# One decode step on one core: V of both head groups in one matmul, row sums as a column of the outputs, output projections in two column tiles

## The chip, the cores and the metric

The kernel runs on one core of one Trainium2 chip. The metric is the device time of one execution in microseconds, the median of three runs. The profile is of one further execution, and carries that execution's own time.

## The reference, cut to what matters

One token for each of 8 batch entries passes through attention over a sliding window and through a gated feed-forward block; both read the same normalised input, and the result gates the one with the other.

```python
xn = layernorm(x)                                  # x: (8, 1, 512) bfloat16
q  = xn @ wq                                       # 32 heads of 128
k, v = the last 1024 positions of k_cache, v_cache # 8 KV heads, each shared by 4 query heads
p  = softmax(q @ k^T * 128**-0.5)
s  = (p @ v) @ wo                                  # 4096 -> 512
f  = (gelu(xn @ w_gate) * (xn @ w_up)) @ w_down    # 512 -> 1792 -> 512
y  = x + s * silu(f)
```

The caches give 8 batch entries x 8 heads x 1024 positions x 128 x 2 bytes, twice: 33.6 MB. wq and wo are 4.2 MB each, the three feed-forward weights 1.8 MB each. Everything has to come from HBM once.

## The kernel before, in words

**Loads.** All large loads are issued by SyncE, in program order, on one DMA queue: wo's first quarter (`wo_first`, line 106), all of wq (line 109), then K and V of one batch entry after the other in halves of 1 MB (`load_cache`, line 84), w_gate and w_up (line 438), w_down (line 441), and the last three quarters of wo (line 451), the last of them in three pieces of 5, 2 and 1 of its 8 slices `j`. K, V and the late weights share a ring of eight slots. x comes on ScalarE's queue in five pieces of 2, 2, 2, 1 and 1 rows (line 79).

**Head.** VectorE normalises x, TensorE transposes it (line 167) and spreads x itself, by a matmul with a 0/1 matrix (line 172), onto the partitions that the result will have; ScalarE keeps that as `x_res` (line 179). Then 32 matmuls make q (line 261), and q is rearranged into `qbd`, a block form of the queries (line 284).

**Loop over the batch.** For each batch entry, `turn_k` transposes K on VectorE (line 249), `scores` makes a 128 x 1024 score tile in PSUM (line 311), `softmax` takes the maximum, the exponential (line 333) and, with the same instruction, the row sums, into the column `sums[:, b]`. `turn_p` transposes the probabilities (line 344). `values` multiplies them with V (line 355): the 32 positions `c` are dealt onto four column tiles of the array, 32 columns each (`t = c % 4`), once for each of the two groups `g` of four KV heads, so 64 matmuls of 128 moving columns. `keep_o` copies the result to SBUF (line 368). `gather`, one entry later, adds the four tiles by matmuls with a selection matrix in float32: two for the outputs (line 376) and two of one column for the sums (line 380). After four entries `regroup` divides by the sums and lays the heads out for wo (lines 391 to 407). The schedule is the program's own order; each engine executes its instructions in that order:

```python
softmax(b); scores(b + 1, 0); gather(b - 1)
turn_k(b + 1, 1); scores(b + 1, 1)
turn_p(b); values(b); keep_o(b)
```

**Tail.** After `gather(7)` and `regroup(1)` come w_gate and w_up (line 465), the gelu (lines 475 to 488), and w_down: for each of 14 slices `j` of 128 rows four matmuls, one for each column tile, with 128 of the 512 output columns each (line 494). The gate `g_sb` follows (lines 502 to 506). Then wo in the same form, 32 slices of four matmuls (line 513), where the loop over the quarters `u` follows the order in which they arrive. At last `y` (line 521), `out_sb` (line 523), and one store of 32 runs of 256 bytes (line 525).

Of the kernel before, what the change touches and what calls it, by code (L numbers as in the profile page):

```python
# [7 lines left out]
ACT = mybir.ActivationFunctionType  # L8
ALU = mybir.AluOpType
AX = mybir.AxisListType  # L10
BF16 = mybir.dt.bfloat16
FP32 = mybir.dt.float32
# [4 lines left out]
RB = 4  # L17
# [4 lines left out]
def kernel(  # L22
# [13 lines left out]
    nc = tc.nc  # L36

    B, Sq, D = A_x.shape
    Hkv, Sk, Dh = A_k_cache.shape[1], A_k_cache.shape[2], A_k_cache.shape[3]
# [6 lines left out]
    P = nc.NUM_PARTITIONS  # L46
    NK = D // P
    HG = 4
    NG = Hkv // HG
    C = W * HG // P  # L50
    ROW = C * Dh
    FT = F // 4
    NJ = F // P
    DT = D // 4

    ctx.enter_context(tc.manual_schedule())
    consts = ctx.enter_context(tc.tile_pool(name="consts", bufs=1))
    keep = ctx.enter_context(tc.tile_pool(name="keep", bufs=1))
    two = ctx.enter_context(tc.tile_pool(name="two", bufs=2))
# [15 lines left out]


    x_sb = keep.tile([B, D], BF16, name="x_sb")
    for r, z in ((0, 2), (2, 4), (4, 6), (6, 7), (7, 8)):
        nc.scalar.dma_start(out=x_sb[r:z], in_=A_x.flatten_outer_dims()[r:z])  # L79

    def load_cache(cache, b, name):
# [10 lines left out]
    k_sb, v_sb = {}, {}  # L92
# [4 lines left out]
    def load_v(b):  # L97
# [21 lines left out]
        out=ident,  # L119
        in_=ident,  # L120
# [13 lines left out]
        out=xpad,  # L134
        in_=xpad,
# [8 lines left out]
    stats = keep.tile([B, nc.vector.BN_STATS_DIM], FP32, name="stats")  # L144
# [3 lines left out]
    rstd = keep.tile([B, 1], FP32, name="rstd")  # L148
# [4 lines left out]
        out=xhat,  # L153
# [3 lines left out]
        op0=ALU.subtract,  # L157
        op1=ALU.mult,
    )
    x_res = keep.tile([P, DT], FP32, name="x_res")  # L160
    warm = keep.tile([B, 1], FP32, name="warm")
    nc.scalar.activation(out=warm, in_=rstd, func=ACT.Exp)  # L162
    with tc.tile_pool(name="ps_x", bufs=1, space=PSUM) as ps_x:
        xnT_ps = ps_x.tile([P, NK, B], BF16, name="xnT_ps")
        xv = xhat.rearrange("b (p k) -> b k p", k=NK)
        for k in range(NK):
            nc.tensor.transpose(xnT_ps[:, k, :], xv[:, k, :], ident[0:B, 0:B])  # L167
        for j in range(4):
            nc.vector.tensor_copy(out=xnR[:, :, j, 0 : RB * B : RB], in_=xnT_ps)
        xr_ps = ps_x.tile([P, DT], FP32, name="xr_ps")  # L170
        for t in range(4):
            nc.tensor.matmul(
                xr_ps[32 * t : 32 * t + 32, :],
                xpad,
                x_sb[:, t * DT : (t + 1) * DT],
                start=True,
                stop=True,
            )
        nc.scalar.copy(out=x_res, in_=xr_ps)  # L179
# [10 lines left out]
        out=hv,  # L190
        in_=hv,
# [7 lines left out]
        out=neg_st,  # L199
        in_=neg_st,  # L200
# [8 lines left out]
        out=neg_mv,  # L209
        in_=neg_mv,  # L210
# [9 lines left out]
    sel = consts.tile([P, NG, Hq], FP32, name="sel")  # L220
    nc.vector.memset(sel, 0.0)
    for g in range(NG):
        nc.vector.tensor_reduce(
            out=sel[:, g, g * qd : (g + 1) * qd],
            in_=ident.rearrange("p (t g h) -> p g h t", t=4, g=NG)[:, g],
# [5 lines left out]
        out=own, in_=ident.rearrange("p (i e) -> p e i", e=8), axis=AX.X, op=ALU.add  # L231
    )
    pick = consts.tile([P, 4 * NU], BF16, name="pick")
    with nc.allow_low_precision(reason="sums of zeros and a single one"):
        nc.vector.tensor_reduce(
            out=pick, in_=ident.rearrange("p (a e) -> p a e", e=8), axis=AX.X, op=ALU.add
# [20 lines left out]
    with tc.tile_pool(name="ps_q", bufs=1, space=PSUM) as ps_q:  # L257
        q_ps = [ps_q.tile([P, 512], FP32, name=f"q_ps{i}") for i in range(8)]
        for k in range(NK):
            for i in range(8):  # L260
# [4 lines left out]
                    start=(k == 0),  # L265
                    stop=(k == NK - 1),
                )
        for half in range(2):
            for i in range(4 * half, 4 * half + 4):
                e = nc.vector.tensor_copy if i % 4 == 3 else nc.scalar.copy  # L270
# [7 lines left out]
    for j in range(4):  # L278
        sl = slice(32 * j, 32 * j + 32)
        for m in range(2):  # L280
            for g in range(NG):
                e = nc.scalar.copy if (4 * j + 2 * m + g) % 3 == 2 else nc.vector.tensor_copy
# [3 lines left out]


    pT, S, P_sb, O_ps = {}, {}, {}, {}
    sums = keep.tile([P, B], FP32, name="sums")

    actx = ExitStack()
    ps_s = actx.enter_context(tc.tile_pool(name="ps_s", bufs=2, space=PSUM))
# [26 lines left out]
    def softmax(b):  # L319
        mx = two.tile([P, 1], FP32, name="mx")  # L320
        nc.vector.tensor_reduce(  # L321
            out=mx, in_=S[b].rearrange("p a c -> p (a c)"), axis=AX.X, op=ALU.max
        )

        m2 = two.tile([64, 1], FP32, name="m2")
        nc.vector.tensor_tensor(out=m2, in0=mx[0:64, :], in1=mx[64:128, :], op=ALU.max)
        m1 = two.tile([32, 1], FP32, name="m1")
        nc.vector.tensor_tensor(out=m1, in0=m2[0:32, :], in1=m2[32:64, :], op=ALU.max)  # L328
        nb = two.tile([P, 1], FP32, name="nb")
        for j in range(4):  # L330
            nc.scalar.mul(nb[32 * j : 32 * j + 32, :], m1, -inv)  # L331
        P_sb[b] = two.tile([P, C // 2, 32, 2], BF16, name="P_sb")
        nc.scalar.activation(  # L333
            out=P_sb[b].rearrange("p c i w -> p c w i"),
            in_=S[b].rearrange("p a (c w i) -> p (a c) w i", w=2, i=32),
            func=ACT.Exp,
            bias=nb,
            scale=inv,
            accum_out=sums[:, b : b + 1],
        )  # L340

    def turn_p(b):
        pT[b] = two.tile([P, C // 2, Hq, 2], BF16, name="pT")
        nc.vector.transpose(  # L344
            out=pT[b].rearrange("p c h w -> p (c h w)").bitcast(I32),
            in_=P_sb[b].rearrange("p c i w -> p (c i w)").bitcast(I32),
        )

    def values(b):
        O_ps[b] = ps_o.tile([P, NG, Dh], FP32, name="O_ps")  # L350
        for g in range(NG):
            vv = v_sb[b][:, g].rearrange("p (c d) -> p c d", d=Dh)
            for c in range(C):
                t = c % 4
                nc.tensor.matmul(  # L355
                    O_ps[b][32 * t : 32 * t + 32, g, :],
                    pT[b][:, c // 2, :, c % 2],
                    vv[:, c, :],
                    start=(c < 4),
                    stop=(c >= C - 4),  # L360
                )

    o_ps = {}
    O_sb = {}

    def keep_o(b):
        O_sb[b] = two.tile([P, NG, Dh], FP32, name="O_sb")
        nc.scalar.copy(out=O_sb[b], in_=O_ps[b])  # L368

    def gather(b):  # L370
        q = b % 4
        if q == 0:
            o_ps[b // 4] = ps_g.tile([P, Dh + 1], FP32, name="o_ps")
        o = o_ps[b // 4][32 * q : 32 * q + 32, :]
        for g in range(NG):
            nc.tensor.matmul(  # L376
                o[:, 0:Dh], sel[:, g, :], O_sb[b][:, g, :], start=(g == 0), stop=(g == NG - 1)
            )
        for g in range(NG):
            nc.tensor.matmul(  # L380
                o[:, Dh : Dh + 1],
                sel[:, g, :],
                sums[:, b : b + 1],
                start=(g == 0),
                stop=(g == NG - 1),
            )

    def regroup(q):

# [53 lines left out]
    for u in range(1, NU):  # L443
        if u % 2 == 1:
            pair = slot("wo_sb").rearrange("p (v j d) -> p v j d", v=2, d=D)
        t = pair[:, (u - 1) % 2]
# [5 lines left out]
        wo.append(t)  # L452

    gather(B - 1)
    regroup(1)
    actx.close()

    ps_f = ctx.enter_context(tc.tile_pool(name="ps_f", bufs=1, space=PSUM))
    ffn = ctx.enter_context(tc.tile_pool(name="ffn", bufs=1))
    zu = []  # L460
    for n, ws in (("z_ps", wgu[0]), ("u_ps", wgu[1])):
        ps = ps_f.tile([P, FT], FP32, name=n)
        for k in range(NK):
            for t in range(4):
# [4 lines left out]
                    start=(k == 0),  # L469
                    stop=(k == NK - 1),  # L470
# [6 lines left out]
        out=z2, in0=z2, scalar1=0.044715, scalar2=1.0, op0=ALU.mult, op1=ALU.add  # L477
# [10 lines left out]
    nc.vector.transpose(  # L488
        out=hT.rearrange("p j b -> p (j b)"), in_=h_bf.rearrange("p (y j) -> p j y", j=NJ)
    )  # L490
    f_ps = ps_f.tile([P, DT], FP32, name="f_ps")
    for j in range(NJ):
        for t in range(4):
            nc.tensor.matmul(
                f_ps[32 * t : 32 * t + 32, :],
                hT[:, j, :],
                wd[:, j, t * DT : (t + 1) * DT],
                start=(j == 0),
                stop=(j == NJ - 1),
            )  # L500
    g_sb = ffn.tile([P, DT], FP32, name="g_sb")
    nc.scalar.activation(out=g_sb, in_=f_ps, func=ACT.Tanh, scale=0.5)
    nc.vector.tensor_scalar(
        out=g_sb, in0=g_sb, scalar1=0.5, scalar2=0.5, op0=ALU.mult, op1=ALU.add
# [1 line left out]
    nc.vector.tensor_tensor(out=g_sb, in0=g_sb, in1=f_ps, op=ALU.mult)  # L506


    s_ps = ps_f.tile([P, DT], FP32, name="s_ps")
    for u in range(NU):  # L510
        for j in range(8):
            for t in range(4):
                nc.tensor.matmul(  # L513
                    s_ps[32 * t : 32 * t + 32, :],
                    oT[:, j, u, :],
                    wo[u][:, j, t * DT : (t + 1) * DT],
                    start=(u == 0 and j == 0),
                    stop=(u == NU - 1 and j == 7),
                )
    y = ffn.tile([P, DT], FP32, name="y")  # L520
    nc.vector.tensor_tensor(out=y, in0=s_ps, in1=g_sb, op=ALU.mult)
    out_sb = ffn.tile([P, DT], BF16, name="out_sb")
    nc.vector.tensor_tensor(out=out_sb, in0=y, in1=x_res, op=ALU.add)
    out_f = out.flatten_outer_dims()
    nc.sync.dma_start(
        out=out_f.rearrange("b (t d) -> t b d", t=4), in_=out_sb[0 : P : RB, :]
    )


# [28 lines left out]
```

## Time and profile before

| | |
|---|---|
| median of 3 runs | 120.95 us (120.84 to 121.92) |
| the profiled execution's own time | 120.88 us |
| its span in the profile | 119.0 us |
| mean granted TensorE clock | 0.887 |
| HBM read | 47.46 MB |
| busy: TensorE, VectorE, ScalarE | 61%, 64%, 26% of the span |
| SyncE's DMA queue | 94.6% of 16 engines' span |
| instructions | 2306, 992 of them matmuls |

Times in the trace are microseconds from the start of the span. "Idle before, releaser" is the time for which an engine did nothing ahead of an instruction, and what ended it. PEclk is the granted TensorE clock as a share of full speed. The matmuls' ends are modelled, their starts are recorded.

### The profile page before, as it was taken

To read this page: it belongs to the slowest core of one execution; us is meant where nothing else is said; L and a number is where in the kernel's file an instruction comes from. 1 tells how busy PE (TensorE), PEld (TensorE's weight loads), DVE (VectorE), ACT (ScalarE), POOL (GpSimd) and SP (SyncE) were. 2 spreads that over 40 slices of the span, in tenths; PEclk is the share of its full clock that TensorE was granted. 3 is DMA by queue.
4 is the path that set the end of the run, shared out by engine and by line. 5 is a ranking of instruction groups with operands and counts; after the bars stand their busy time and mean duration, and the time that the engine had idled before them with its cause. 6 is when DMAs were issued, how large, how long until landed. Compare 5 with 4: busy or idle time off the path is not lost.

```text
span 119.0 us, 2306 instructions
## 1 busy us (share of the span) xinstructions
PE 72.0 (61%) x992; PEld 37.5 (32%) x992; DVE 75.8 (64%) x101; ACT 31.4 (26%) x75; POOL 3.2 (3%) x10
## 2 busy tenths in 40 slices
PE   0000079941599596979964875698399264844650
PEld 0000033410133253545532434244135253414530
DVE  1000487999999999999957995971994224165100
ACT  1300230096202417170531421151070800120000
POOL 2000052000000000000000000000000000000000
PEclk9999999999679999999999999689859955578595
DMA  2998999999999999999999999999999999999930
GB/s 72 458 507 375 391 421 424 435 427 427 427 430 419 424 435 419 427 430 416 432 424 424 421 430 427 419 435 421 427 424 427 440 434 430 419 431 416 415 138 3
DMA packets 6109, 47.60 MB, mean 400 GB/s; under 512 B 716, under 2 KB 852, under 8 KB 1108
## 3 DMA queue, kind: packets, MB, share of 16 engines
q1 hardware_dynamic: 6084, 47.46, 94.6%
q8 instruction: 7, 0.11, 0.3%
q14 instruction: 2, 0.02, 0.0%
q10 hardware_dynamic: 16, 0.01, 0.0%
HBM read 47.46 MB, written 0.01 MB: 399 GB/s over the span
## 4 chain that ended last, share of the span: by engine, by line
DMA 61%; DVE 15%; PE 15%; ACT 3%; issue 2%; ACTq 1%; DVEq 0%
DMA wo_sb<-in_A_wo_dram 19%; DMA k_sb<-in_A_k_cache_dram 17%; DMA v_sb<-in_A_v_cache_dram 17%; DMA x_sb<-in_A_x_dram 9%; PE q_ps L261 7%; PE S_ps L311 6%; DVE kT L249 6%; DVE qbd L284 2%; DVE mx L321 2%; DVE q_both L274 1%; ACT P_sb L333 1%; ACTq L79 1%; ACT L162 1%; DVE q_both L271 1%; PE O_ps L355 1%
## 5 line engine op out<-in xcount | busy, mean ns | idle before, releaser
L311 PE MATMUL S_ps<-kT,qbd 128*128 128x512 bf16 x128 | 34.8, 420 | 15.4 <-DVE kT L249 12.0
L249 DVE STREAM_TRANSPOSE kT<-k_sb 128x2048 int32<-128x2048 int32 x16 | 36.6, 2289 | 5.0 <-DMA k_sb<-in_A_k_cache_dram 4.9
L311 PEld LDWEIGHTS <-qbd 128*128 128x128 bf16 x128 | 13.0, 103 | 33.3 <-issue 18.0
L331 ACT ACTIVATE nb<-m 32x1 f32<-32x1 f32 x32 | 6.4, 201 | 22.9 <-DVE m L328 22.6
L333 ACT ACTIVATE P_sb<-S_ps,nb 128x1024 bf16<-128x1024 f32 x8 | 11.1, 1391 | 0.3
L355 PE MATMUL O_ps<-v_sb,pT 128*32 128x128 bf16 x512 | 9.5, 231 | 2.6 <-DVE pT L344 2.6
L321 DVE TENSOR_REDUCE mx<-S_ps 128x1 f32<-128x1024 f32 x8 | 9.6, 1195 | 1.7 <-PE S_ps L311 1.6
L355 PEld LDWEIGHTS <-pT 128*32 128x32 bf16 x512 | 8.0, 103 | 5.6 <-issue 3.0
L261 PE MATMUL q_ps<-wq_sb,xnR 128*128 128x512 bf16 x32 | 9.2, 460 | 0.5 <-ACT x_res L179 0.5
L167 PE MATMUL xnT_ps<-ident,xhat 8*128 8x8 bf16 x4 | 0.3, 174 | 15.0 <-DVE xhat L152 15.0
L368 ACT COPY O_sb<-O_ps 128x256 f32<-128x256 f32 x8 | 3.0, 372 | 23.7 <-PE O_ps L355 23.7
L145 DVE BATCH_NORM_STATS2 stats<-x_sb 8x6 f32<-8x512 bf16 x1 | 0.7, 683 | 11.8 <-DMA x_sb<-in_A_x_dram 11.8
L344 DVE STREAM_TRANSPOSE pT<-P_sb 128x512 int32<-128x512 int32 x8 | 5.7, 711 | 3.4 <-ACT P_sb L333 3.3
L376 PE MATMUL o_ps<-O_sb,sel 128*32 128x128 f32 x32 | 5.4, 296 | 1.0 <-ACT O_sb L368 1.0
L300 PE MATMUL S_ps<-neg_mv,neg_st 128*128 128x512 bf16 x16 | 4.8, 381 | 1.9 <-DVE q_both L271 1.9
L261 PEld LDWEIGHTS <-xnR 128*128 128x128 bf16 x32 | 3.6, 114 | 5.8 <-issue 3.0
L271 ACT CAST q_both<-q_ps 128x512 bf16<-128x512 f32 x6 | 3.0, 613 | 7.9 <-PE q_ps L261 7.9
L167 PEld LDWEIGHTS <-xhat 8*128 8x128 bf16 x4 | 0.2, 114 | 15.0 <-DVE xhat L152 15.0
L376 PEld LDWEIGHTS o_ps<-O_sb,sel 128*32 128x32 f32 x32 | 3.0, 115 | 4.7 <-issue 3.2
L513 PE MATMUL s_ps<-wo_sb,oT 128*32 128x128 bf16 x96 | 2.7, 252 | 2.2 <-DMA wo_sb<-in_A_wo_dram 2.2
L252 DVE MEMSET qbd<- 128x4096 uint32 x1 | 3.5, 3472 | 0.8 <-issue 0.8
L513 PEld LDWEIGHTS <-oT 128*32 128x32 bf16 x128 | 3.0, 123 | 2.8 <-issue 2.6
(65 smaller groups left out, 51.1 us busy)
## 6 DMA issues: line engine op xcount, KB each, us to landing
k_sb<-in_A_k_cache_dram SPq DMA_DIRECT2D x16, 1024.0 KB, 19.7
v_sb<-in_A_v_cache_dram SPq DMA_DIRECT2D x16, 1024.0 KB, 19.8
wq_sb<-in_A_wq_dram SPq DMA_DIRECT2D x1, 4096.0 KB, 14.2
wo_sb<-in_A_wo_dram SPq DMA_DIRECT2D x2, 1024.0 KB
wgu_sb<-in_B_w_gate_dram SPq DMA_DIRECT2D x1, 1792.0 KB
wgu_sb<-in_B_w_up_dram SPq DMA_DIRECT2D x1, 1792.0 KB
wd_sb<-in_B_w_down_dram SPq DMA_DIRECT2D x1, 1792.0 KB, 25.1
wo_first<-in_A_wo_dram SPq DMA_DIRECT2D x1, 1024.0 KB, 4.8
```

What stands on the lines that cost most here:

```text
L249: nc.vector.transpose(out=t.bitcast(I32), in_=k_sb[b][:, g].bitcast(I32))
L261: nc.tensor.matmul(q_ps[i], xnR[:, k, :, :].rearrange("p j b -> p (j b)"), wq_sb[k][:, i * 512 : (i + 1) * 512], start=(k == 0), stop=(k = ...
L271: e(out=q_bf[:, i * 512 : (i + 1) * 512], in_=q_ps[i])
L300: nc.tensor.matmul(S[b][:, half, :], neg_st.rearrange("p j h -> p (j h)"), neg_mv.rearrange("p a n -> p (a n)"), start=True, stop=False,)
L311: nc.tensor.matmul(S[b][:, half, :], qbd[:, m, b, w, g, :], kv[:, half * 16 : (half + 1) * 16, m, :, w], start=False, stop=(g == NG - 1 an ...
L321: nc.vector.tensor_reduce(out=mx, in_=S[b].rearrange("p a c -> p (a c)"), axis=AX.X, op=ALU.max)
L331: nc.scalar.mul(nb[32 * j : 32 * j + 32, :], m1, -inv)
L333: nc.scalar.activation(out=P_sb[b].rearrange("p c i w -> p c w i"), in_=S[b].rearrange("p a (c w i) -> p (a c) w i", w=2, i=32), func=ACT.Exp,
L344: nc.vector.transpose(out=pT[b].rearrange("p c h w -> p (c h w)").bitcast(I32), in_=P_sb[b].rearrange("p c i w -> p (c i w)").bitcast(I32),)
L355: nc.tensor.matmul(O_ps[b][32 * t : 32 * t + 32, g, :], pT[b][:, c // 2, :, c % 2], vv[:, c, :], start=(c < 4), stop=(c >= C - 4),)
L376: nc.tensor.matmul(o[:, 0:Dh], sel[:, g, :], O_sb[b][:, g, :], start=(g == 0), stop=(g == NG - 1))
L513: nc.tensor.matmul(s_ps[32 * t : 32 * t + 32, :], oT[:, j, u, :], wo[u][:, j, t * DT : (t + 1) * DT], start=(u == 0 and j == 0), stop=(u = ...
```

## The change

1. **x in four pieces** of two rows each instead of five.
2. **Values.** One matmul of 256 moving columns (both head groups side by side) replaces two of 128: 32 for each batch entry instead of 64. The four column tiles stay.
3. **Sums.** `O_sb` becomes 129 columns wide for each group. The exponential writes its row sums straight into the last column of group 0, a new ScalarE copy of 128 x 1 puts them in group 1, `keep_o` fills the other columns, and `gather` needs two matmuls of 129 columns instead of two of 128 and two of one. `O_sb` is therefore taken from its two buffers in `softmax(b)`, no longer in `keep_o(b)`.
4. **w_down, wo and the result in two column tiles.** `DT` is 256 instead of 128: `x_res`, `f_ps`, `g_sb`, `s_ps`, `y` and `out_sb` have 64 partitions of 256 columns, and each slice `j` takes two matmuls of 256 columns instead of four of 128.
5. **The store** is two plain ones of 8 runs of 512 bytes, one issued by SyncE, one by ScalarE.
6. The table load ahead of the first exponential is drawn by an activation that writes into `stats` instead of a tile of its own.

```diff
-    DT = D // 4
+    NT = 2
+    DT = D // NT
-    for r, z in ((0, 2), (2, 4), (4, 6), (6, 7), (7, 8)):
+    for r, z in ((0, 2), (2, 4), (4, 6), (6, 8)):
         nc.scalar.dma_start(out=x_sb[r:z], in_=A_x.flatten_outer_dims()[r:z])
...
-    nc.scalar.activation(out=warm, in_=rstd, func=ACT.Exp)
+    nc.scalar.activation(out=stats[:, 0:1], in_=rstd, func=ACT.Exp)
...
+        O_sb[b] = two.tile([P, NG, Dh + 1], FP32, name="O_sb")
         nc.scalar.activation(out=P_sb[b]..., func=ACT.Exp,
-            accum_out=sums[:, b : b + 1],
+            accum_out=O_sb[b][:, 0, Dh : Dh + 1],
         )
+        nc.scalar.copy(out=O_sb[b][:, 1, Dh : Dh + 1], in_=O_sb[b][:, 0, Dh : Dh + 1])
...
-        for g in range(NG):
-            vv = v_sb[b][:, g].rearrange("p (c d) -> p c d", d=Dh)
-            for c in range(C):
-                t = c % 4
-                nc.tensor.matmul(O_ps[b][32 * t : 32 * t + 32, g, :],
-                    pT[b][:, c // 2, :, c % 2], vv[:, c, :], ...)
+        vv = v_sb[b].rearrange("p g (c d) -> p c g d", d=Dh)
+        for c in range(C):
+            t = c % 4
+            nc.tensor.matmul(O_ps[b][32 * t : 32 * t + 32, :, :],
+                pT[b][:, c // 2, :, c % 2], vv[:, c, :, :], ...)
...
-        nc.scalar.copy(out=O_sb[b], in_=O_ps[b])
+        nc.scalar.copy(out=O_sb[b][:, :, 0:Dh], in_=O_ps[b])
...
-            nc.tensor.matmul(o[:, 0:Dh], sel[:, g, :], O_sb[b][:, g, :], ...)
-        for g in range(NG):
-            nc.tensor.matmul(o[:, Dh : Dh + 1], sel[:, g, :], sums[:, b : b + 1], ...)
+            nc.tensor.matmul(o, sel[:, g, :], O_sb[b][:, g, :], ...)
...
     for j in range(NJ):
-        for t in range(4):
+        for t in range(NT):
             nc.tensor.matmul(f_ps[32 * t : 32 * t + 32, :], hT[:, j, :], wd[:, j, t * DT : (t + 1) * DT], ...)
...
     for u in range(NU):
         for j in range(8):
-            for t in range(4):
+            for t in range(NT):
                 nc.tensor.matmul(s_ps[32 * t : 32 * t + 32, :], oT[:, j, u, :], wo[u][:, j, t * DT : (t + 1) * DT], ...)
...
-    nc.sync.dma_start(
-        out=out_f.rearrange("b (t d) -> t b d", t=4), in_=out_sb[0 : P : RB, :]
-    )
+    for t, e in ((0, nc.sync), (1, nc.scalar)):
+        e.dma_start(
+            out=out_f[:, t * DT : (t + 1) * DT], in_=out_sb[32 * t : 32 * t + 32 : RB, :]
+        )
```

More of the change, by code (lines that the diff above doesn't have):

```diff
@@ L159 @@
     )
-    x_res = keep.tile([P, DT], FP32, name="x_res")
-    warm = keep.tile([B, 1], FP32, name="warm")
-    nc.scalar.activation(out=warm, in_=rstd, func=ACT.Exp)
+    x_res = keep.tile([32 * NT, DT], FP32, name="x_res")
+    nc.scalar.activation(out=stats[:, 0:1], in_=rstd, func=ACT.Exp)
     with tc.tile_pool(name="ps_x", bufs=1, space=PSUM) as ps_x:
@@ L169 @@
             nc.vector.tensor_copy(out=xnR[:, :, j, 0 : RB * B : RB], in_=xnT_ps)
-        xr_ps = ps_x.tile([P, DT], FP32, name="xr_ps")
-        for t in range(4):
+        xr_ps = ps_x.tile([32 * NT, DT], FP32, name="xr_ps")
+        for t in range(NT):
             nc.tensor.matmul(
@@ L288 @@
     pT, S, P_sb, O_ps = {}, {}, {}, {}
-    sums = keep.tile([P, B], FP32, name="sums")
     actx = ExitStack()
@@ L350, in values @@
         O_ps[b] = ps_o.tile([P, NG, Dh], FP32, name="O_ps")
-        for g in range(NG):
-            vv = v_sb[b][:, g].rearrange("p (c d) -> p c d", d=Dh)
-            for c in range(C):
-                t = c % 4
[L355 to L360, printed above, removed]
-                )
+        vv = v_sb[b].rearrange("p g (c d) -> p c g d", d=Dh)
+        for c in range(C):
+            t = c % 4
+            nc.tensor.matmul(
+                O_ps[b][32 * t : 32 * t + 32, :, :],
+                pT[b][:, c // 2, :, c % 2],
+                vv[:, c, :, :],
+                start=(c < 4),
+                stop=(c >= C - 4),
+            )
     o_ps = {}
@@ L366, in keep_o @@
     def keep_o(b):
-        O_sb[b] = two.tile([P, NG, Dh], FP32, name="O_sb")
-        nc.scalar.copy(out=O_sb[b], in_=O_ps[b])
+        nc.scalar.copy(out=O_sb[b][:, :, 0:Dh], in_=O_ps[b])
     def gather(b):
@@ L375, in gather @@
         for g in range(NG):
-            nc.tensor.matmul(
-                o[:, 0:Dh], sel[:, g, :], O_sb[b][:, g, :], start=(g == 0), stop=(g == NG - 1)
-            )
-        for g in range(NG):
[L380 to L386, printed above, removed]
+            nc.tensor.matmul(o, sel[:, g, :], O_sb[b][:, g, :], start=(g == 0), stop=(g == NG - 1))
     def regroup(q):
@@ L490 @@
     )
-    f_ps = ps_f.tile([P, DT], FP32, name="f_ps")
+    f_ps = ps_f.tile([32 * NT, DT], FP32, name="f_ps")
     for j in range(NJ):
-        for t in range(4):
+        for t in range(NT):
             nc.tensor.matmul(
@@ L500 @@
             )
-    g_sb = ffn.tile([P, DT], FP32, name="g_sb")
+    g_sb = ffn.tile([32 * NT, DT], FP32, name="g_sb")
     nc.scalar.activation(out=g_sb, in_=f_ps, func=ACT.Tanh, scale=0.5)
@@ L506 @@
     nc.vector.tensor_tensor(out=g_sb, in0=g_sb, in1=f_ps, op=ALU.mult)
-    s_ps = ps_f.tile([P, DT], FP32, name="s_ps")
+    s_ps = ps_f.tile([32 * NT, DT], FP32, name="s_ps")
     for u in range(NU):
         for j in range(8):
-            for t in range(4):
+            for t in range(NT):
                 nc.tensor.matmul(
@@ L519 @@
                 )
-    y = ffn.tile([P, DT], FP32, name="y")
+    y = ffn.tile([32 * NT, DT], FP32, name="y")
     nc.vector.tensor_tensor(out=y, in0=s_ps, in1=g_sb, op=ALU.mult)
-    out_sb = ffn.tile([P, DT], BF16, name="out_sb")
+    out_sb = ffn.tile([32 * NT, DT], BF16, name="out_sb")
     nc.vector.tensor_tensor(out=out_sb, in0=y, in1=x_res, op=ALU.add)
     out_f = out.flatten_outer_dims()
-    nc.sync.dma_start(
-        out=out_f.rearrange("b (t d) -> t b d", t=4), in_=out_sb[0 : P : RB, :]
-    )
+    for t, e in ((0, nc.sync), (1, nc.scalar)):
+        e.dma_start(
+            out=out_f[:, t * DT : (t + 1) * DT], in_=out_sb[32 * t : 32 * t + 32 : RB, :]
+        )
 _INS = ['A_x', 'A_k_cache', 'A_v_cache', 'A_wq', 'A_wo', 'B_x', 'B_w_gate', 'B_w_up', 'B_w_down']
```

## The prediction

> **What bounds the kernel.** I read the page's slices first, then the queues, then the timeline of the tail.
>
> ```profile
> DVE  1000487999999999999957995971994224165100
> DMA  2998999999999999999999999999999999999930
> GB/s 72 458 507 375 391 421 424 435 427 427 427 430 419 424 435 419 427 430 416 432 424 424 421 430 427 419 435 421 427 424 427 440 434 430 419 431 416 415 138 3
> q1 hardware_dynamic: 6084, 47.46, 94.6%
> q8 instruction: 7, 0.11, 0.3%
> DMA 61%; DVE 15%; PE 15%; ACT 3%; issue 2%; ACTq 1%; DVEq 0%
> ```
>
> From the second to the last slice but two, the DMA engines are full; 94.6% of 119.0 us is 112.6 us of packets on SyncE's queue, between the first near 2 us and the last at 115.06 us. No compute engine is full. The chain of waits runs through x, q and K, but it only follows who released whom: a 1 MB half of K or V takes 19.7 us from issue to landing while the queue moves 1 MB in 2.45 us, so about seven more loads are queued ahead of it. An issue could come some 17 us later before an engine ran dry. So nothing inside the loop sets the end; the stream of 47.46 MB does, and what follows its last byte:
>
> ```profile
> 108.80 1.35 PE L494 MATMUL f_ps<-wd_sb,hT 128*32 128x128 bf16 x56 [3.33 <-DVE hT L488]
> 109.92 1.08 PE L513 MATMUL s_ps<-wo_first,oT 128*32 128x128 bf16 x32
> 110.78 1.08 PE L513 MATMUL s_ps<-wo_sb,oT 128*32 128x128 bf16 x32
> 112.92 0.63 PE L513 MATMUL s_ps<-wo_sb,oT 128*32 128x128 bf16 x32 [1.06 <-DMA wo_sb<-in_A_wo_dram]
> 114.47 0.46 PE L513 MATMUL s_ps<-wo_sb,oT 128*32 128x128 bf16 x20 [0.92 <-DMA wo_sb<-in_A_wo_dram]
> 115.11 0.57 PE L513 MATMUL s_ps<-wo_sb,oT 128*32 128x128 bf16 x12 [0.18 <-DMA wo_sb<-in_A_wo_dram]
> 115.73 0.29 DVE L521 TENSOR_TENSOR y<-s_ps,g_sb 128x128 f32<-128x128 f32 x1 [4.61 <-PE s_ps L513]
> 116.06 0.29 DVE L523 TENSOR_TENSOR out_sb<-y,x_res 128x128 bf16<-128x128 f32 x1
> 116.38 0.70 SPq L525 DMA_DIRECT2D out_dram<-out_sb  x1
> ```
>
> TensorE is ahead of the stream: it waits for each of the last wo pieces. The last wait ends at 115.44 us (the recorded start of the last four matmuls). From there: 0.24 matmuls, 0.29, 0.29, 0.70 issue, 0.6 to the first store packet (117.68), 0.17 of packets, 0.35 until SyncE sees it (118.21), and the program's closing.
>
> **Part by part, against the profiled 120.88 us** (0.07 under the median).
>
> *x in four pieces.* A two-row piece puts one row on each of two engines (packets at 6.479 and 6.482 us), a one-row piece goes to one (8.95, then 11.41; its completion write at 12.66). Each packet waits some 1.2 us behind a 32 KB packet of wq. With four pieces the last completion is that of today's fourth, 10.20 us, so x lands 2.46 us earlier. q gains only up to wq's landing at 15.09 us plus about 0.4 until an engine sees it, against a q start of 16.03: 0.5 us. It frees slots earlier, which a full queue can't use: 0.
>
> *V in 256 columns.* At full clock 64 matmuls of 128 columns on four tiles take 1.08 us: 16 rounds x 53 ns and 0.22 for the last to drain. New: 8 rounds x 107 ns and some 0.27. The columns stay the same: +0.05 us for an entry, inside the loop, 0 for the end. The first matmul now needs both halves of V. The last half of entry 7 is complete at 94.83 us and `values(7)` starts at 96.05; slack about 0.8 even with the time to see it.
>
> *Sums.* Gone are 32 one-column matmuls with their loads. In entry 7 the next scores start at 89.37 us, held by them for 0.2 us; after `gather(7)` they keep `rc` from 99.48 until 99.69. Both are on the chain from the last K to f_ps: that chain gains 0.37 and loses 0.05 to V, so f_ps starts at 108.48 instead of 108.80 (w_down is there at 107.62 + 0.4). The new 128x1 copy, about 0.2 us by the nb row (201 ns), follows the exponential on ScalarE; next there is keep_o, which waits for V 2.75 us in entry 7. Uncovered it would cost 0.2 of these 0.32. The new wait of the exponential for `gather(b-2)` is met before the scores it needs.
>
> *Two column tiles.* Here work is added. A round of four 128-column matmuls starts every 55 ns at full clock (112.972, 113.027, 113.082) and every 107 ns at half (32 matmuls, 109.92 to 110.78). Two tiles of 256 columns need two such rounds for each slice: 109 and 213 ns. 46 slices (14 of w_down, 32 of wo) go from 2.5 to 5.0 us at full clock, from 4.9 to 9.8 at half. The clock in the tail:
>
> ```profile
> 106.00:107.00 1.00, 0.00 (x0) 0.00 (x0) 0.97 (x2) 0.00 (x0) 0.00 (x0) 1.00 0.97 414
> 109.60:110.00 0.40, 0.40 (x27) 0.40 (x20) 0.00 (x0) 0.00 (x0) 0.00 (x0) 0.50 1.12 471
> 111.50:112.00 0.50, 0.36 (x16) 0.18 (x5) 0.00 (x0) 0.00 (x0) 0.00 (x0) 0.50 0.90 379
> 113.00:114.00 1.00, 0.55 (x32) 0.40 (x32) 0.00 (x0) 0.00 (x0) 0.00 (x0) 1.00 0.73 279
> ```
>
> The seventh column is the clock: full until 109.20, half until 112.62, full after. New, with the same changes: 0.72 us at full are 6.7 slices; f_ps done at 110.75; wo's first quarter at 112.46; the second, mostly at full, at 113.39; the third (there at 112.92) at 114.24; the piece of five waits for 114.47 as today. **TensorE just catches up, with 0.2 us to spare**, and only the last pair costs: 256 columns instead of 128, +0.05.
>
> The clock's steps, twelve in the trace, all lie whole multiples of 3.413 us after the first at 20.457 us. The Trainium skill (TensorE: Matmul & The Clock Gate, "What's actually happening") says that this window runs free and doesn't start with the kernel. By that rule the step at 112.62 can lie elsewhere in another execution, and the backlog show in the time; no trace here shows a second phase.
>
> *y and out_sb* have 256 elements for each partition. 128 take 292 ns, 448 take 621 (lines 479 to 485): 1.03 ns each, so 0.42 each, +0.26 us in all. Nothing hides it.
>
> *Stores.* The 32 runs cost 0.70 us of issue. The x loads of one or two rows cost 0.24 to 0.27, ScalarE's first 0.54, loads of 128 runs 0.33 to 0.5. For 8 runs the bounds are 0.24 and, with a cold ScalarE queue as dear as today's store, 0.70 and 0.24 more. I take 0.54, nearest being ScalarE's own first: -0.16. Old packets lie on four engines, eight of 15 to 18 ns on each: 0.17; one 512-byte packet lies between that and 46 ns (1024 bytes): -0.12. One more event that SyncE waits for at the end: +0.06.
>
> The Trainium skill (DMA: Bandwidth & Descriptors, "Specifications") puts the smallest transfer at full rate at 512 bytes, with a read-modify-write below; by it the change would win at the store. The trace differs: a 256-byte write took 15 to 18 ns against 46 for a 1024-byte read, so it has at most the 0.12 to give.
>
> *Instructions.* TensorE loses 382 matmuls and as many weight loads (256 V, 32 sums, 28 w_down, 64 wo, 2 x_res), of 992 pairs. Its code comes in the seven 16 KB packets of the instruction queue, each on another DMA engine. In the completion writes each throws its engine back by 1.41 us: the 16 writes of one load spread over 0.56 us at 29 us, and over 1.81 at 105. The last engine sets the end of the stream. About four packets remain; by the engines of the first four, whose writes went to 1.66, 1.57, 1.66 and 1.70, the last landing is 0.1 earlier. Bounds: -1.2 (no late engine), +0.2 (the last of the unhit ones is hit, 0.56 + 1.41).
>
> **Sum:** -0.10 stream, +0.05 last matmuls, +0.26 VectorE, -0.16 and -0.12 store, +0.06 event = -0.01. **120.9 us, no change**; its own range by the bounds of stream and store 120.4 to 121.4.
>
> **Rivals.**
>
> *TensorE becomes the last (slower).* It decides where the 43 slices due by 115.11 us don't fit into the 6.6 us after 108.48, that is, where over 4.1 us of these are at half clock; today's steps give 3.4. With other positions of the steps and a window counted as busy from about 75% on (2.66 of 3.41 us were followed by full clock, 2.44 by half), I get up to +0.75: 121.1 to 121.7. If the clock stayed at half throughout, 46 x 0.213 = 9.8 us end at 118.3 plus draining, 2.7 later: 123.6. Against it: the window ahead of 112.62 is filled better than before. For it: only 0.2 us to spare.
>
> *The stream ends earlier (faster).* If no packet of code hits an engine that is late already, up to 1.2 us: 119.7. Against: seven out of seven left their mark.
>
> *The loop was the bound after all,* as the chain has it: q's 0.5 us would reach the end, 120.4. Against: the full DMA row.
>
> *The change saves nothing on TensorE*, since 256 columns stream as long as two times 128. I hold that to be so; a gain from fewer instructions in the loop would need an idle DMA.
>
> **Chances.** Forecast 0.63; TensorE last for part of a window 0.15 (121.1 to 121.7); at half clock throughout 0.10 (123.6); stream earlier 0.07 (119.7); loop 0.03; a dearer second store 0.02 (122.2). A measurement of this kernel tells about 1% (1.2 us) from no change. Faster 0.07; slower 0.10 + 0.02 and 0.01 from the phases = 0.13; same 0.80. Range 120.2 to 121.9: it leaves out the stream's case, the half clock throughout and the store.
>
> **What would show it.** V 32 matmuls in some 1.1 us; q start near 15.5; f_ps starting near 108.5 and taking 2.3 to 2.6 us; wait for wo_sb ahead of the last pieces kept but shorter than 0.9; y and out_sb 0.42; issue under 0.55. Wrong, if the last matmuls wait for no DMA, or the last completion write moves by over 0.3 us.

## The result and the profile after

The changed kernel takes **121.43 us** (median of 22 runs, 121.20 to 121.85), the kernel before 120.94 us (median of 22). The ratio is 1.0033, with a 95% interval of 1.0019 to 1.0046: slower by 0.4 us in the ratio, 0.49 in the medians, where I had forecast no change.

From the page of the changed kernel, slices and queues as before:

```profile
DMA  2998999999999999999999999999999999999920
GB/s 69 459 506 374 393 420 426 437 423 426 426 431 417 423 434 428 423 420 437 428 417 423 434 420 428 426 437 423 417 431 431 436 442 419 428 420 423 403 83 3
q1 hardware_dynamic: 6064, 47.45, 94.4%
q8 instruction: 5, 0.08, 0.2%
DMA 60%; PE 23%; DVE 9%; ACT 3%; issue 1%; SPq 0%; DVEq 0%
```

The DMA engines are as full as before in every slice up to the last but two. The instruction packets (q8) went from seven to five. The chain of waits now has PE 23% where it had 15%: it no longer reaches the end through the last wo load, but through w_down's and wo's matmuls. The timeline of the tail says the same (start, duration, engine and line; in brackets idle time before and what ended it):

```profile
108.23 3.17 PE L483 MATMUL f_ps<-wd_sb,hT 128*32 128x256 bf16 x28 [2.82 <-DVE hT L477]
111.19 1.53 PE L502 MATMUL s_ps<-wo_first,oT 128*32 128x256 bf16 x16
112.56 3.02 PE L502 MATMUL s_ps<-wo_sb,oT 128*32 128x256 bf16 x48
115.62 0.42 DVE L510 TENSOR_TENSOR y<-s_ps,g_sb 64x256 f32<-64x256 f32 x1 [2.96 <-PE s_ps L502]
116.07 0.42 DVE L512 TENSOR_TENSOR out_sb<-y,x_res 64x256 bf16<-64x256 f32 x1
116.51 0.80 SPq L515 DMA_DIRECT2D out_dram<-out_sb  x1
116.52 0.75 ACTq L515 DMA_DIRECT2D out_dram<-out_sb  x1
```

Against the rows of before: wo's matmuls stand in one block without a marked wait for a load; `y` and `out_sb` take 0.42 us each instead of 0.29; the issue of a store takes 0.80 and 0.75 us, not the 0.54 of my estimate, and not even less than the 0.70 of before. f_ps's row takes 3.17 us, where I had said 2.3 to 2.6, since the clock in this execution was half until 112.20 us. The last byte of wo is complete at 114.95 us (115.06 before), the last two matmuls start at 115.29 (115.44), out_sb ends at 116.49 (116.35), and the span ends at 119.34 (119.02). So the changed kernel is 0.15 us ahead when TensorE sees the last load, 0.14 behind at the end of out_sb, and 0.32 behind at the end: **all of the loss lies behind the last load**, some 0.3 us in front of the store and some 0.2 in it. The store's part, from the end of out_sb on, is made up as follows: SyncE's issue 0.10 longer, its first packet 0.78 us after the issue's end instead of 0.61, its packets 0.09 shorter, and the rest, from its last completion write to the end of the span, as before. This profiled execution took 121.20 us and is one of the two fastest of the 22; why most take 0.2 us more is a question for the runs below.

### The profile page after: what moved, and what is told of

Read it like the earlier page. It is cut to its first block, busy times and chain, and to the rows that moved or that the text cites. A ratio compares the mean times of both kernels' runs of the same rounds, so it can differ in the third digit from the quotient of the medians.

```text
span 119.3 us, 1553 instructions
## 1 busy us (share of the span) xinstructions
PE 73.7 (62%) x610; PEld 35.1 (29%) x610; DVE 76.3 (64%) x101; ACT 33.1 (28%) x83; POOL 3.2 (3%) x10
## 4 chain that ended last, share of the span: by engine, by line
DMA 60%; PE 23%; DVE 9%; ACT 3%; issue 1%; SPq 0%; DVEq 0%
DMA k_sb<-in_A_k_cache_dram 48%; DMA wq_sb<-in_A_wq_dram 12%; PE q_ps L261 8%; PE S_ps L310 4%; PE s_ps L502 4%; PE f_ps L483 3%; DVE kT L249 2%; PE O_ps L355 2%; PE z_ps L454 1%; PE o_ps L375 1%; ACT P_sb L333 1%; DVE o_x L382 1%; DVE mx L320 1%; DVE hT L477 1%; ACT nb L330 1%
## 5 line engine op out<-in xcount | busy, mean ns | idle before, releaser
L355 PE MATMUL O_ps<-v_sb,pT 128*32 128x256 bf16 x256 | 9.3, 292 | 2.7 <-DVE pT L345 2.7
L355 PEld LDWEIGHTS <-pT 128*32 128x32 bf16 x256 | 6.5, 102 | 6.3 <-issue 3.0
L375 PE MATMUL o_ps<-O_sb,sel 128*32 128x129 f32 x32 | 5.5, 297 | 1.0 <-ACT O_sb L367 1.0
L483 PE MATMUL f_ps<-wd_sb,hT 128*32 128x256 bf16 x28 | 3.2, 419 | 2.8 <-DVE hT L477 2.8
L502 PEld LDWEIGHTS <-oT 128*32 128x32 bf16 x64 | 3.6, 107 | 0.9
```

Source lines behind the costliest of these rows:

```text
L355: nc.tensor.matmul(O_ps[b][32 * t : 32 * t + 32, :, :], pT[b][:, c // 2, :, c % 2], vv[:, c, :, :], start=(c < 4), stop=(c >= C - 4),)
L375: nc.tensor.matmul(o, sel[:, g, :], O_sb[b][:, g, :], start=(g == 0), stop=(g == NG - 1))
L483: nc.tensor.matmul(f_ps[32 * t : 32 * t + 32, :], hT[:, j, :], wd[:, j, t * DT : (t + 1) * DT], start=(j == 0), stop=(j == NJ - 1),)
L502: nc.tensor.matmul(s_ps[32 * t : 32 * t + 32, :], oT[:, j, u, :], wo[u][:, j, t * DT : (t + 1) * DT], start=(u == 0 and j == 0), stop=(u = ...
```

## The experiments

Two theories were to be told apart. S: the constant parts behind the last load, the wider `y` and `out_sb` and the two stores, make the loss. T: TensorE, with half of its column tiles, is late in part of the executions.

**One store instead of two** (changed kernel, SyncE alone).

```diff
-    for t, e in ((0, nc.sync), (1, nc.scalar)):
-        e.dma_start(out=out_f[:, t * DT : (t + 1) * DT], in_=out_sb[32 * t : 32 * t + 32 : RB, :])
+    nc.sync.dma_start(
+        out=out_f.rearrange("b (t d) -> t b d", t=NT), in_=out_sb[0 : 32 * NT : RB, :])
```

> The changed kernel with one store again, issued by SyncE: 16 runs of 512 bytes, both column tiles. Theory S (the stores): in the two profiles the stretch from the end of out_sb to the end of the span went from 2.67 to 2.85 us, where I had forecast 0.22 less. If the second store and its queue cost that, this run is 0.15 to 0.25 us under the changed kernel (121.43), near 121.2, and the stretch is 2.7 us or less. Theory T (TensorE late in part of the executions, by the position of the clock's steps): no change, 121.4, and executions spread as widely (0.4 us between most). If the issue costs 0.8 us whatever the store looks like, 121.4 too, but then the profile shows one issue of 0.8 us.

Measured: 121.22 us (11 runs), 1.0025 of before (1.0016 to 1.0034). 0.2 us under the changed kernel: S.

```profile
116.68 0.69 SPq L514 DMA_DIRECT2D out_dram<-out_sb  x1
```

The issue took 0.69 us with the same number of 512-byte runs, and from out_sb's end to the span's end it is 2.74 us (changed kernel: 2.86; before: 2.67). Of the 0.24 us left over before, 0.07 lie behind out_sb, most of it one more semaphore that SyncE looks at after the store's; the rest is not the store's.

**Two stores in the kernel before.**

```diff
-    nc.sync.dma_start(out=out_f.rearrange("b (t d) -> t b d", t=4), in_=out_sb[0 : P : RB, :])
+    for h, e in ((0, nc.sync), (1, nc.scalar)):
+        e.dma_start(
+            out=out_f[:, 2 * h * DT : 2 * (h + 1) * DT].rearrange("b (t d) -> t b d", t=2),
+            in_=out_sb[64 * h : 64 * h + 64 : RB, :])
```

> The kernel before with its store cut in two, one half issued by SyncE, one by ScalarE (16 runs of 256 bytes each), and nothing else. Theory S: 0.15 to 0.25 us above the kernel before, 121.1 to 121.2, with a first store packet later by 0.2 to 0.4 us. Theory T: no change, 120.95, since TensorE is ahead of the stream with four column tiles.

Measured: 121.28 us (12 runs), 1.0031 (1.0017 to 1.0046): +0.3, S again, and more than expected. Its tail, from the timeline:

```profile
115.84 0.29 DVE L521 TENSOR_TENSOR y<-s_ps,g_sb 128x128 f32<-128x128 f32 x1 [4.12 <-PE s_ps L513]
116.16 0.29 DVE L523 TENSOR_TENSOR out_sb<-y,x_res 128x128 bf16<-128x128 f32 x1
116.48 0.68 SPq L526 DMA_DIRECT2D out_dram<-out_sb  x1
116.48 0.64 ACTq L526 DMA_DIRECT2D out_dram<-out_sb  x1
```

Counted from out_sb's end, issues and packets are no later than with one store: the first store packets at 117.77 and 117.81 us, the last completion write at 118.00, 1.55 us after out_sb's end against 1.50 before. My expectation of a first packet later by 0.2 to 0.4 us was wrong. The time goes after that: SyncE sees the completion 0.50 us after the write (before: 0.36), and then has three more events to go through, 0.06 us each, since it waits for its semaphores in a fixed order and the store's was the last one in the kernel before. These three come to 0.16 us, about half of what this run lost; in the changed kernel the later store's semaphore is the last again, so that part says nothing about its loss.

**Everything but the two column tiles and the two stores.**

```diff
-    NT = 2
+    NT = 4
...
-    for t, e in ((0, nc.sync), (1, nc.scalar)):
-        e.dma_start(out=out_f[:, t * DT : (t + 1) * DT], in_=out_sb[32 * t : 32 * t + 32 : RB, :])
+    nc.sync.dma_start(
+        out=out_f.rearrange("b (t d) -> t b d", t=NT), in_=out_sb[0 : 32 * NT : RB, :])
```

> The changed kernel with four column tiles of 128 for w_down, wo, x_res and the result, and the one store of before; x in four pieces, V in 256 columns and the sums column stay. Both theories: the loss is gone. By the steps: the last byte lands 0.1 us earlier, nothing is added, 120.8 (120.6 to 121.0). If V, the sums or the new wait cost something in the loop after all, it stays above 121.1.

Measured: 121.00 us (11 runs), 1.0001 (0.9992 to 1.0009). The loss is gone, as both theories say; the 0.1 to 0.2 us of gain that I expected isn't there. Its timeline shows why four tiles don't care:

```profile
108.07 1.69 PE L483 MATMUL f_ps<-wd_sb,hT 128*32 128x128 bf16 x56 [2.57 <-DMA wd_sb<-in_B_w_down_dram]
109.52 1.09 PE L502 MATMUL s_ps<-wo_first,oT 128*32 128x128 bf16 x32
110.50 0.69 PE L502 MATMUL s_ps<-wo_sb,oT 128*32 128x128 bf16 x32
112.94 0.63 PE L502 MATMUL s_ps<-wo_sb,oT 128*32 128x128 bf16 x32 [1.75 <-DMA wo_sb<-in_A_wo_dram]
114.46 1.24 PE L502 MATMUL s_ps<-wo_sb,oT 128*32 128x128 bf16 x32 [0.89 <-DMA wo_sb<-in_A_wo_dram]
```

f_ps starts 0.7 us earlier than in the kernel before, now held by w_down's load, and TensorE waits 1.75 us for wo's third quarter instead of 1.06. The clock was full in the last scores of this profile and half in those of before, so not all of the 0.7 us need be the change's. V in 256 columns, the sums column and the earlier x buy idle time, nothing else. The last load is complete at 115.03 us, against 115.06.

**TensorE with room** (the changed kernel without wo's first quarter).

```diff
-    for u in range(NU):
+    for u in range(1, NU):
...
-                    start=(u == 0 and j == 0),
+                    start=(u == 1 and j == 0),
```

> The changed kernel without the 16 matmuls of wo's first quarter (that part of the projection is left out, its load stays): TensorE gets 0.9 to 1.7 us of room ahead of the last wo pieces, and nothing else changes. Theory T: the executions in which TensorE was late lose 0.1 to 0.5 us; median near 121.2, the value of the best executions of the changed kernel, and a spread as narrow as before's (0.2 us). Theory S: no change, 121.4.

Measured: 121.42 us (5 runs, 121.37 to 121.50), 1.0041 (1.0029 to 1.0053). No change of the median: **T falls as the cause of the median's loss.** TensorE now waits for each piece again:

```profile
113.01 1.05 PE L502 MATMUL s_ps<-wo_sb,oT 128*32 128x256 bf16 x16 [0.60 <-DMA wo_sb<-in_A_wo_dram]
114.52 1.22 PE L502 MATMUL s_ps<-wo_sb,oT 128*32 128x256 bf16 x16 [0.46 <-DMA wo_sb<-in_A_wo_dram]
```

The five runs spread over 0.13 us, the 22 of the changed kernel over 0.65, so the slowest executions may still be T's. The profiled execution of this run took 121.37 us: the last load is complete at 115.12 us, the last matmuls start at 115.45, out_sb ends at 116.64, and from there it takes 2.87 us. The changed kernel's profiled execution, 0.17 us faster, differs from it mainly in the last load (114.95), which is probably what made it one of the fastest.

**TensorE without room** (w_down's matmuls twice).

```diff
+    for again in range(2):
         for j in range(NJ):
             for t in range(NT):
                 nc.tensor.matmul(f_ps[32 * t : 32 * t + 32, :], ...)
```

> The changed kernel with w_down's 28 matmuls run twice into the same sums (the second pass starts over, so the result is the same): TensorE gets 14 more slices ahead of wo, 1.5 us at full clock, 3.0 at half. In the profile of the changed kernel TensorE reached the piece of five at 114.36 us with under 0.1 us of waiting. If TensorE stands at the edge there, nearly all of it appears in the time: 122.8 to 124.4, and no matmul waits for a wo load any more. If there was hidden room, less than 0.8 us appears.

Measured: 123.16 us (4 runs, 121.79 to 123.31), 1.0143 (1.0095 to 1.0191). Of some 2.2 us of additional matmuls (the row of w_down takes 5.34 us instead of 3.17), 1.7 reach the median; in one run of the four, 121.79 us, only 0.4 did. From its timeline:

```profile
108.53 5.34 PE L484 MATMUL f_ps<-wd_sb,hT 128*32 128x256 bf16 x56 [3.07 <-DVE hT L477]
113.70 1.04 PE L503 MATMUL s_ps<-wo_first,oT 128*32 128x256 bf16 x16
114.57 2.79 PE L503 MATMUL s_ps<-wo_sb,oT 128*32 128x256 bf16 x48
117.40 0.42 DVE L511 TENSOR_TENSOR y<-s_ps,g_sb 64x256 f32<-64x256 f32 x1 [2.28 <-PE s_ps L503]
```

No wo matmul waits for a load, and the last start at 117.08 us, while the last load is complete at 115.09. So T's mechanism is real, and in most executions its price begins right behind where the changed kernel stands. The run at 121.79 us hid over 1 us of the added work; there is no profile of it, but its mean granted clock, 0.900, was the highest of the four.

**A warm queue** (kernel before, with a small copy on SyncE's queue ahead of the store).

```diff
+    wk = ffn.tile([1, 64], FP32, name="wk")
+    nc.sync.dma_start(out=wk, in_=g_sb[0:1, 0:64])
     y = ffn.tile([P, DT], FP32, name="y")
```

> The kernel before, with one more issue on SyncE's queue some 4 us ahead of the store: 256 bytes of g_sb copied into a tile that nobody reads. Theory C (cold queue): the store's issue costs 0.70 us, where loads of x cost 0.24, because SyncE has issued nothing for 20 us; then it falls to 0.3 to 0.5 us and the time by 0.2 to 0.4, 120.6 to 120.8. Theory F (an issue of a store costs this much, whatever came before): still 0.70 us, 120.95, or a little more for one more completion to wait for.

Measured: 121.28 us (12 runs), 1.0019 (1.0007 to 1.0032). The small copy was issued at 111.48 us, 0.62 us long, and the store's issue is as it was:

```profile
111.48 0.62 SPq L521 DMA_DIRECT2D wk<-g_sb  x1
112.95 0.63 PE L513 MATMUL s_ps<-wo_sb,oT 128*32 128x128 bf16 x32 [0.77 <-DMA wo_sb<-in_A_wo_dram]
...
116.37 0.72 SPq L527 DMA_DIRECT2D out_dram<-out_sb  x1
```

A queue idle for 20 us is not the reason; theory C falls. The added 0.3 us is not the copy itself, long done: in the profile the stretch behind out_sb is 2.85 us instead of 2.67, as the store's semaphore again isn't the last in SyncE's order; the rest of the added time lies outside the span and stays unexplained. Three of the twelve runs, with the same span, took 120.92 to 120.95 us.

**The first store alone** (changed kernel, right half not written).

```diff
-    for t, e in ((0, nc.sync), (1, nc.scalar)):
+    for t, e in ((0, nc.sync),):
```

> The changed kernel with SyncE's store alone: the right half of the result is not written. If the second store costs by its own completion and by standing beside the first, the issue falls from 0.80 to 0.70 us or less, the stretch from the end of out_sb to the end of the span from 2.86 to 2.65, and the time to 121.2. If a store of 8 runs on eight engines is dear by itself, the issue stays at 0.8 us, and only the second completion (0.06 to 0.2 us) goes: 121.25 to 121.4.

Measured: 121.23 us (12 runs), 1.0021 (1.0010 to 1.0033). Mixed, as neither sentence foresaw:

```profile
116.78 0.80 SPq L515 DMA_DIRECT2D out_dram<-out_sb  x1
```

The issue stays at 0.80 us with nobody beside it, but the first packet comes 0.61 us after it again, the stretch falls to 2.74 us and the time by 0.2 us, the same as with one store of both halves. So the second store costs about 0.2 us, and the dear issue of the eight-engine store is paid back by its packets (first to last start in 0.06 us instead of 0.16).

This run's profile also holds a case of theory T (the columns of the stretches: their length, then busy time and instructions of PE, PEld, DVE, ACT and POOL, granted clock, DMA share, GB/s):

```profile
112.00:113.00 1.00, 1.00 (x14) 0.69 (x11) 0.41 (x1) 0.00 (x0) 0.00 (x0) 0.50 0.97 395
113.00:114.00 1.00, 1.00 (x18) 0.84 (x16) 0.00 (x0) 0.00 (x0) 0.00 (x0) 0.79 0.73 277
115.00:115.60 0.60, 0.60 (x16) 0.53 (x12) 0.00 (x0) 0.00 (x0) 0.00 (x0) 1.00 0.01 2
```

The full clock comes at 113.42 us, 1.2 us later than in the changed kernel's profile (112.20). TensorE is busy without a gap, the last matmuls start one pair after the other, 109 ns apart, until 115.57, although the last load was complete at 115.05 and would have let them start at 115.4. So this execution lost 0.1 to 0.2 us to TensorE: 121.35 us against a median of 121.23.

**The store on ScalarE's queue** (as the four-tile kernel above).

```diff
-    nc.sync.dma_start(
+    nc.scalar.dma_start(
         out=out_f.rearrange("b (t d) -> t b d", t=NT), in_=out_sb[0 : 32 * NT : RB, :])
```

> The changed kernel with four column tiles and one store, this store issued by ScalarE instead of SyncE. In the runs with two stores ScalarE's issue took 0.05 us less than SyncE's (0.64 against 0.68, 0.75 against 0.80). If that is all that differs, 0.05 us under the same kernel with SyncE's store (121.0), about 120.95, which a measurement can't tell from no change; if ScalarE's queue costs something of its own, 121.1 or more.

Measured: 120.90 us (12 runs, 120.84 to 120.97), 0.9993 (0.9983 to 1.0004). The issue took 0.64 us instead of 0.70. It is the lowest median of all, but can't be told from the kernel before.

**Two column tiles alone** (kernel before, one store).

```diff
-    DT = D // 4
+    NT = 2
+    DT = D // NT
...   (x_res, f_ps, g_sb, s_ps, y, out_sb with 32 * NT partitions; loops over t in range(NT))
```

> The kernel before with two column tiles and nothing else: one store by SyncE, V, sums and x as before. f_ps starts at 108.8 instead of the 108.0 to 108.2 of the changed kernel. If y and out_sb are the whole price of the two tiles (0.25 us, and 0.05 for the last matmul): 121.2 to 121.3, as the changed kernel with one store (121.22). If TensorE is at the edge in the tail, the earlier start of f_ps that V and the sums give is what pays for its doubled time there, and without it 0.2 to 0.6 us are added: 121.4 to 121.8.

Measured: 121.28 us (12 runs, 121.14 to 122.15), 1.0026 (1.0004 to 1.0049). The median fits `y`, `out_sb` and the last matmuls as the whole price. Whether the earlier f_ps pays for the two tiles stayed open here: in the profiled execution f_ps began at 107.97 us without V's and the sums' help, held only by w_down's load, because the clock was full in the scores and V's matmuls that lead to it (full from 80.24 to 97.30 us; in the kernel before half from 85.31 to 88.72 and from 95.55 on). V's matmuls of the last entry took 1.08 us there, against 1.90 before. The chain to f_ps varies by more between executions than the change gives it.

## Why the prediction was wrong

The sum was -0.10 stream, +0.05 last matmuls, +0.26 VectorE, -0.16 and -0.12 store, +0.06 event = -0.01. Measured: **0.0 stream, +0.05, +0.25, and +0.2 for the stores together = +0.5**, against the medians' 0.49.

- **The step that failed is "Stores".** I forecast 0.22 us of gain, and the store lost 0.2 (changed kernel against the same with one store: 121.43 and 121.22). The working took the issue for something that falls with the number of runs, and took ScalarE's first load of x, 0.54 us, as the nearest row. The runs show (a store's engines counted by its completion writes) 0.64 to 0.69 us for 16 runs on two engines, be they of 256 or 512 bytes, 0.64 to 0.72 for 32 runs on four, and 0.75 to 0.80 for 8 runs on eight: fewest runs, dearest issue. No row of a load bore on it. The upper bound that I gave, 0.70 and 0.24 more, was high enough for the issue, but nothing in the sum stood for what two stores cost after it. In the profiles with two stores, the second one's completion either came later (1.68 and 1.78 us after out_sb's end, against 1.48 to 1.52 with one store) or was seen later (0.50 and 0.52 us after its write, against 0.34 to 0.36). What delays it was not found. So the rival of a dearer second store, to which I gave 0.02, is the one that came, with 0.2 us of loss where I had priced it at 1.3.
- **The packets** of each store were right: 0.06 us from first to last instead of 0.16. Eight engines bought that with 0.1 us more of issue. But the two stores' packets did not come together: in the changed kernel's profile ScalarE's started at 117.91 us and SyncE's at 118.09, so both took 0.24 us.
- **The stream.** Five code packets, not the four forecast, and the last load complete at 114.95 us looked like the 0.1 that I forecast. But the other runs with five such packets have it at 115.03 to 115.11, the run without wo's first quarter, with four of them, at 115.12, and the kernel before at 115.06: the gain is 0 within what executions differ by. The bound of -1.2 left out that two 8 KB packets of another queue of instructions (33.8 and 61.6 us in the kernel before) set an engine back too, by 0.84 and 0.55 us.
- **y and out_sb**: forecast 0.42 each, measured 0.416 and 0.418. Four tiles against two, one store each: 121.00 and 121.22. This step is right, and it is half of the loss.
- **V, sums, x.** V's matmuls of one entry took 1.06 us (1.08 before; forecast 1.13), x's last completion came at 10.26 us (forecast 10.20), q started at 15.63 (forecast 15.5), f_ps at 108.23 (forecast 108.48). None of it reached the end, as forecast: four tiles with all of it measured 1.0001. The rival that took the chain of waits for the bound is refuted: x landed 2.4 us earlier and the time didn't move.
- **Two column tiles.** A slice took 213 ns at half clock and 109 at full, as forecast. TensorE came to the piece of five with under 0.1 us of waiting; I had said 0.2 to spare. The rival that it becomes the last one did happen in single executions, by 0.1 to 0.2 us in the one profiled, and doesn't make the median. The mean granted clocks of the executions point the same way: the five of the changed kernel under 0.875 have a median of 121.59 us, the other 17 one of 121.40; with two tiles alone it is 121.68 (three) against 121.21 (nine). The 75 executions of the kernel before that ran beside the experiments show no such gap (120.93 us under 0.875, 120.98 above), but the same kernel with two stores shows one of 0.13, so this is a hint and not a proof. My limit for this rival, 4.1 us at half clock, should have been 4.0 by the same numbers. That the clock's step can lie elsewhere is shown: the steps lie whole multiples of 3.413 us apart in every profile, but the one to full clock in the tail came at 112.20, 113.42, 112.88, 111.56, 111.26 and 110.96 us in the profiled two-tile kernels. Here the traces agree with the rule of the Trainium skill (TensorE: Matmul & The Clock Gate, "What's actually happening") of a window that runs free.
- **512 bytes.** A 512-byte packet took 25 to 27 ns (32 or 33 for the first two in the runs with one store of 16) where a 256-byte one took 15 to 18, so twice the bytes per packet saved some 10 ns in every pair of old packets. That is all that the runs show of the 512-byte rule of the Trainium skill (DMA: Bandwidth & Descriptors, "Specifications").
- **The range** (120.2 to 121.9) held the time. The bounds for the store reached from about -0.6 to +0.3 us; it was the choice inside them that gave the wrong side.

## What to carry to other kernels

When a full DMA stream sets the end, count only what lies behind its last byte, and count it to the last semaphore: fewer matmuls, shorter chains and earlier loads ahead of it turned into idle time here, while 0.12 us on each of two VectorE instructions and a second store's completion came through in full. A result spread over more partitions was cheaper in the last elementwise steps (128 x 128 took 0.29 us, 64 x 256 took 0.42), and for these 8 KB one store beat two on two queues. Halving the column tiles doubled TensorE's time for the same product (55 to 109 ns for a slice at full clock); check it against the clock's slow half before calling it covered.

## What the runs showed of the hardware

- The time of a store's issue rose with the engines that it was dealt to, while runs and bytes went the other way or stayed: two engines 0.68 to 0.69 us on SyncE, four 0.70 to 0.72, eight 0.80; ScalarE's was 0.04 to 0.07 us shorter each time. An idle queue is not the reason (0.72 us with an issue 5 us earlier). No run varied engines and runs apart.
- At the end SyncE goes through its semaphores in a fixed order, 0.06 us for each. If the store's semaphore isn't the last of them, those behind it are paid after it: 0.16 us where three stood behind it, 0.06 where one did, for a change that looks as if it touched nothing else.
- Code is a load too: each 16 KB packet of instructions set one DMA engine back by 1.4 us in its completion writes, and five or four packets instead of seven didn't bring the last landing forward (114.95 to 115.12 us with five or four, 115.06 to 115.22 with seven). That one late engine is enough for it would fit this; no run had none.
